# Attention with slot routing on one core: all attention products as plain fp32 in 64x64 array tiles, logits and slot work once per batch

## The chip, the cores and the metric

The kernel runs on one core of a Trainium2 chip. The metric is the device time of one execution in microseconds (us). TensorE (PE in the profile) does the products, VectorE (DVE) and ScalarE (ACT) the elementwise work, SyncE (SP) issues the DMAs; PEld is TensorE's loading of the stationary operand.

## The reference

Attention with a sigmoid in place of a softmax, followed by a soft mixture of experts over all tokens of all batches (8 batches, 12 heads, 448 tokens, head size 64; 3584 tokens of width 768; 32 slots, 8 experts of 4 slots, hidden width 1024), all in float32:

```python
scores = scale * np.matmul(q, k.transpose(0, 1, 3, 2)) - np.log(S)
attn = 1.0 / (1.0 + np.exp(-scores))
x = np.matmul(attn, v)            # then (B*S, H*D)

logits = x @ phi                  # (3584, 32)
d = softmax(logits, axis=0)       # over all tokens
slot_input = d.T @ x              # (32, 768), 4 rows per expert
slot_out[e] = relu(slot_input[e] @ w1[e]) @ w2[e]
c = softmax(logits, axis=1)       # over the slots
return c @ slot_out
```

The softmax over all tokens is kept as a running maximum and a running sum over the batches.

## The kernel before

*Attention loop* (lines 332 to 365). It runs over 48 pairs of heads (8 batches of 6 pairs). Both heads of a pair lie on the 128 partitions, 64 each. For each pair, `load_qk` brings 448 KB of q and k, `load_v` 224 KB of v. `split` (L122) cuts q and k on DVE into a rounded fp32r part and a remainder; `qk_step` (L133) adds three fp32r products per head for each of four chunks of 112 keys (high by high, high by low, low by high), 64 rows by 112 columns of the array, and lets ACT take the sigmoid (L141). `av_step` (L144) multiplies the result with v in plain fp32, 112 rows by 64 columns, both heads beside one another, adding over the four chunks. `evac` (L151) copies the sum out of PSUM, `turn` (L155) transposes it in 32x32 blocks for the slot job.

In the loop's order, PE does for pair p: the scores, then `logits_job` of pair p-1 (L161: four products that write 32 slots by up to 128 tokens each), then the weighted sums of pair p. DVE then splits pair p+1.

*Once per batch.* `softmax_a`, `softmax_b`, `softmax_r`, `softmax_c` (L169 to L205) work on a batch's logits during the first two pairs of the next batch. `spread` (L207) writes the weights to DRAM (`zd`) and reads them back in another order with four DMAs (`dr`). In the third pair, `slot_job` (L245) does 56 small products in 32x32 tiles (L235) and DVE adds them to `acc`. `last_job` (L256) does the same for the last batch without DRAM.

*Tail* (from L373). `w1_part` and `h_part` do the first expert layer, the `hf` loop the second, and `out_batch` (L476) the combination, whose results go to DRAM by L487.

*Order.* PE, SP, DVE and ACT run in the order in which the program is written. All loads and stores go through SP's one queue: an instruction of it that waits holds up all behind it. Weights come in 128 units of 384 KB through a ring: 56 buffers (`wa`, N_A) are filled during attention by L335, 13 more (`wb`, N_B) lie in the memory that attention leaves, and later units wait until an earlier one was read.

Of the kernel before, what the change touches and what calls it, by code (L numbers as in the profile page):

```python
# [18 lines left out]
P = 128  # L19
CH = 112  # L20
NCH = S // CH
# [6 lines left out]
N_B = 13  # L28
# [5 lines left out]
NLT = B // 2  # L34
# [7 lines left out]
def soft_moe_attention(ctx: ExitStack, tc: tile.TileContext, qk, v, phi, w1, w2, cst, out):  # L42
# [14 lines left out]
    lt_all = cpool.tile([P, NLT, P], F32, name="lt_all")  # L57
# [33 lines left out]
    ps_lg = ctx.enter_context(tc.tile_pool(name="ps_lg", bufs=1, space=PSUM))  # L91
    lg_all = ps_lg.tile([P, 512], F32, name="lg").rearrange("p (b t) -> p b t", b=NLT)
    nc.vector.memset(lg_all, NEG)

    def lg_of(b):
        return lg_all[:, b % NLT, :]

    with ExitStack() as actx:
        ldq = actx.enter_context(tc.tile_pool(name="ldq", bufs=1))
        ldv = actx.enter_context(tc.tile_pool(name="ldv", bufs=2))  # L100
        sp = actx.enter_context(tc.tile_pool(name="sp", bufs=1))
        at = actx.enter_context(tc.tile_pool(name="at", bufs=1))
        xp = actx.enter_context(tc.tile_pool(name="xp", bufs=1))
        bounce = actx.enter_context(tc.tile_pool(name="bounce", bufs=2, space=bass.MemoryType.DRAM))
        ps_sc = actx.enter_context(tc.tile_pool(name="ps_sc", bufs=3, space=PSUM))
        ps_av = actx.enter_context(tc.tile_pool(name="ps_av", bufs=1, space=PSUM))

        qkts, vts, splits, av, xTs, ys, dts, drs = {}, {}, {}, {}, {}, {}, {}, {}
# [7 lines left out]
        def load_v(p):  # L116
            if p < NP:
                t = ldv.tile([CH, NCH, P], F32, name="vt")
                nc.sync.dma_start(t[:], v[p])
                vts[p] = t  # L120

        def split(p, i, z, copy=nc.vector.tensor_copy):  # L122
            if z == 0:
                splits[p, i] = sp.tile([P, 2, S], F32R, name=("qs", "ks")[i])
            dst, src = splits[p, i], qkts[p][:, i * S:(i + 1) * S]
            if z == 0:
                copy(dst[:, 0, :], src)  # L127
            else:
                nc.vector.tensor_tensor(out=dst[:, 1, :], in0=src, in1=dst[:, 0, :].bitcast(F32), op=ALU.subtract)  # L129

        atts = {}

        def qk_step(p, c):  # L133
            qs, ks = splits[p, 0], splits[p, 1]
            sc = ps_sc.tile([P, 2, 512], F32, name="sc")
            for z, y in ((0, 0), (0, 1), (1, 0)):
                for h, r in enumerate(heads):
                    nc.tensor.matmul(  # L138
                        sc[0:CH, h, 0:S], ks[r, z, c * CH:(c + 1) * CH], qs[r, y, :], start=(z + y == 0), stop=(z == 1))
            att = at.tile([CH, 2, S], F32, name=f"att{c}")  # L140
            nc.scalar.activation(att[:], sc[0:CH, :, 0:S], AF.Sigmoid, bias=nbias[0:CH, :], scale=QSCALE)  # L141
            atts[p, c] = att

        def av_step(p, c):  # L144
            if c == 0:
                av[p] = ps_av.tile([P, 512], F32, name="av")
            for h, r in enumerate(heads):
                nc.tensor.matmul(  # L148
                    av[p][r, 0:S], vts[p][:, c, r], atts[p, c][:, h, :], start=(c == 0), stop=(c == NCH - 1))

        def evac(p, copy=nc.vector.tensor_copy):  # L151
            xTs[p] = xp.tile([P, S], F32, name="xT", bufs=3)
            copy(xTs[p][:], av[p][:, 0:S])  # L153

        def turn(p):  # L155
            b, hp = divmod(p, NPR)
            if hp == 0:
                ys[b] = xp.tile([P, NPR, S], F32, name="y")
            nc.vector.transpose(ys[b][:, hp, :], xTs[p][:])  # L159

        def logits_job(p):  # L161
            b, hp = divmod(p, NPR)
            for j in reversed(range(4)):
                n = P if j < 3 else S - 3 * P
                nc.tensor.matmul(  # L165
                    lg_of(b)[32 * j:32 * j + 32, 0:n], phi_sb[:, hp, :], xTs[p][:, j * P:j * P + n],
                    start=(hp == 0), stop=(hp == NPR - 1))

        def softmax_a(b):  # L169
            t1 = small.tile([P, 2, 132], F32, name="t1")  # L170
            zt, ls = t1[:, 0, :], lg_of(b)
# [9 lines left out]
            if b < NLT:  # L181
                nc.vector.transpose(lt_all[:, b, :], ls)
# [8 lines left out]
        def softmax_r(b):  # L191
# [5 lines left out]
        def softmax_c(b):  # L197
            pe = dts[b][:, 1, :]
            if b == 0:
                nc.vector.tensor_reduce(out=mz[:, 1:2], in_=pe[:, 0:P], axis=AX.X, op=ALU.add)  # L200
            else:
# [3 lines left out]
                    out=mz[:, 1:2], in0=mz[:, 1:2], scalar=pe[:, P:P + 1], in1=zb[:], op0=ALU.mult, op1=ALU.add)  # L205

        def spread(b):  # L207
            z = dts[b][:, 0, 0:P]
            nc.vector.transpose(z, dts[b][:, 1, 0:P])
            flat = bounce.tile([P, P], F32, name="zd")  # L210
            nc.sync.dma_start(flat[:], z)
# [16 lines left out]
        def slot_mm(b):  # L228
            sl = [ps_sc.tile([P, 2, 512], F32, name="sc") for _ in range(2)]
            y = ys[b]  # L230
            for c in range(NBK):
                for a in range(4):
                    for j in range(4 if c < 2 else 3):
# [4 lines left out]
                            y[32 * a:32 * a + 32, :, k * BLK:(k + 1) * BLK],  # L238
# [17 lines left out]
        def last_job(b):  # L256
            lg = lg_of(b)
# [5 lines left out]
            pa = ps_sc.tile([P, 2, 512], F32, name="sc")  # L263
            pw = ps_av.tile([P, 512], F32, name="av")

            def warm(n):
                for _ in range(n):
                    nc.tensor.matmul(pw[:, 0:P], ident, ident, start=True, stop=True)
# [7 lines left out]
            nc.tensor.matmul(pa[0:1, 0, 0:P], m1[:, 1:2], ident, start=True, stop=True)  # L276
            warm(2)
            widen(b, pe)
            mrow = small.tile([1, 1, NSLOT], F32, name="mrow")
            nc.vector.tensor_reduce(  # L280
                out=mrow[:], in_=pa[0:1, 0, 0:P].rearrange("o (j s) -> o s j", j=4), axis=AX.X, op=ALU.max)
            unwiden(b, ps_sc.tile([P, 2, 512], F32, name="sc")[:, 0, :])
            for j in range(4):
                nc.tensor.matmul(pa[32 * j:32 * j + 32, 1, 0:1], mrow[:, 0, :], csb[0:1, 0:1], start=True, stop=True)
            warm(1)
            sl = slot_mm(b)
            nc.vector.tensor_tensor(out=cw[:, 2:3], in0=m1[:, 1:2], in1=pa[:, 1, 0:1], op=ALU.subtract)
            nc.scalar.activation(cw[:, 3:4], cw[:, 2:3], AF.Exp)
            nc.vector.tensor_scalar(sw, sel4, cw[:, 3:4], None, op0=ALU.mult)
            total = sp.tile([P, DM], F32, name="qs")  # L290
# [7 lines left out]
            ps = ps_av.tile([P, 512], F32, name="av")  # L298
# [3 lines left out]
            nc.vector.tensor_copy(sT[:].rearrange("p k s -> p (k s)"), ps[:, 0:NKC * NSLOT])  # L302
            nc.vector.tensor_reduce(out=cw[:, 4:5], in_=pe, axis=AX.X, op=ALU.add)
# [13 lines left out]
        load_v(0)  # L317
        nc.sync.dma_start(csb[:], cst)
        nc.sync.dma_start(phi_sb, phi)
        load_v(1)  # L320
        pw = ps_av.tile([P, 512], F32, name="av")
        for _ in range(WARM):
            nc.tensor.matmul(pw[:, 0:WN], acc[:, 0:P], acc[:, 0:WN], start=True, stop=True)  # L323
        dmy = small.tile([1, 1], F32, name="dmy")
        nc.scalar.activation(dmy[:], nbias[0:1, :], AF.Sigmoid)
        split(0, 0, 0)
        split(0, 1, 0, nc.scalar.copy)
        split(0, 0, 1)
        split(0, 1, 1)
        load_qk(1)  # L330

        for p in range(NP):
            b, hp = divmod(p, NPR)
            edge, after, third, fourth = (b > 0 and hp == i for i in range(4))
            while state["next"] < min(N_A, (p + 1) * N_A // 40):  # L335
                load_unit()
            if p > 0:
                evac(p - 1)
            if after:
                softmax_r(b - 1)  # L340
                softmax_c(b - 1)
                spread(b - 1)
            for c in range(NCH):
                qk_step(p, c)
            if p > 0:
                logits_job(p - 1)
                if fourth:
                    turn(p - 3)
                    turn(p - 2)
                if not (after or third):  # L350
                    turn(p - 1)
            if edge:
                softmax_a(b - 1)
                softmax_b(b - 1)
            for c in range(NCH):
                av_step(p, c)
            if p + 1 < NP:
                split(p + 1, 0, 0)
                split(p + 1, 0, 1)
                split(p + 1, 1, 0)  # L360
                split(p + 1, 1, 1)
            load_qk(p + 2)
            load_v(p + 2)
            if third:
                slot_job(b - 1)
        dmx = small.tile([1, 1], F32, name="dmx")
        nc.scalar.activation(dmx[:], atts[NP - 1, 3][0:1, 0, 0:1], AF.Exp)
        evac(NP - 1)
        logits_job(NP - 1)
        turn(NP - 1)  # L370
        finish = last_job(B - 1)
# [55 lines left out]
    def logits_turn(b):  # L427
        nc.vector.transpose(lt_all[:, b % NLT, :], lg_of(b))

# [133 lines left out]
```

## Time and profile before

| what | value |
|---|---|
| three runs, us | 447.48, 447.72, 449.42 (median 447.72) |
| span of the profiled execution, us | 445.2 |
| PE / DVE / ACT busy, us | 405.3 / 224.4 / 215.9 |
| mean granted TensorE clock | 0.971 |
| first score product to end of the last weighted sum, us from the start | 5.16 to 326.64 |
| mean DMA rate over the span | 219 GB/s |

For the profiled execution the page gives its span, the time from its first to its last instruction, and no other time; the runs were measured by themselves. In the rows, a group is a line of the kernel on one engine: its busy time, the mean time of one instruction, and the idle time before it with what ended it. Matmuls overlap one another in the array, so the mean of one is longer than the spacing of two.

### The profile page before, as it was taken

What the parts mean: (1) busy time and instruction counts of PE and PEld (TensorE: products, weight loads), DVE (VectorE), ACT (ScalarE), POOL (GpSimd) and SP (SyncE); (2) the same over time, 40 slices, a digit from 0 to 9 for tenths busy, and PEclk for the clock granted to TensorE, in tenths of its full rate; (3) what the DMA queues carried; (4) which work ended last, traced back from release to release, by engine and by line L of the source; (5) the groups of instructions that cost most, each with busy time, mean ns of one, the idle gap of its engine ahead of it and who ended that gap; (6) DMA issues with size and microseconds to landing.
All of it is one profiled execution on the core that took longest, in us unless ns stands there. A gap on an engine that the chain in (4) does not pass through costs nothing.

```text
span 445.2 us, 9802 instructions
## 1 busy us (share of the span) xinstructions
PE 405.3 (91%) x4026; PEld 208.6 (47%) x4026; DVE 224.4 (50%) x511; ACT 215.9 (48%) x299; POOL 2.4 (1%) x12
## 2 busy tenths in 40 slices
PE   8999999999999999999999999999989988798700
PEld 6554454455554454554554545545545543343500
DVE  3545546556563657455474637475533447351800
ACT  5655645763664556556636736555540115442600
POOL 0000000000000000000000000000011000000000
PEclk9999999999999999999999999999999999989865
DMA  5666646656656565655566655433317999999997
GB/s 180 201 182 217 197 141 214 228 175 197 218 167 194 165 212 195 212 182 186 170 193 230 195 164 197 124 90 128 99 37 254 403 400 402 400 401 399 297 287 234
DMA packets 44541, 97.54 MB, mean 219 GB/s; under 512 B 4688, under 2 KB 16592, under 8 KB 44496
## 3 DMA queue, kind: packets, MB, share of 16 engines
q1 hardware_dynamic: 44496, 96.91, 65.4%
q8 instruction: 32, 0.52, 0.5%
q14 instruction: 13, 0.11, 0.1%
HBM read 85.43 MB, written 11.47 MB: 218 GB/s over the span
## 4 chain that ended last, share of the span: by engine, by line
PE 75%; DVE 8%; DMA 7%; issue 3%; ACT 2%; SPq 1%; DVEq 0%; ACTq 0%
PE av L148 31%; PE sc L138 28%; PE lg L165 4%; PE ph L399 3%; PE sc L235 3%; DMA zd<-t 2%; DMA qkt<-in_qk_dram 2%; DMA wa<-in_w_dram 2%; PE po L506 1%; PE pt L416 1%; PE ph L484 1%; PE av L323 1%; SPq L214 1%; DMA out_dram<-wa 1%; DVE tmp L412 1%
## 5 line engine op out<-in xcount | busy, mean ns | idle before, releaser
L141 ACT ACTIVATE att<-sc,nbias 112x896 f32<-112x896 f32 x192 | 177.8, 1008 | 138.5 <-PE sc L138 138.5
L148 PE MATMUL av<-att,vt 112*64 112x448 f32 x768 | 154.9, 545 | 0.0
L138 PE MATMUL sc<-qs,ks 64*112 64x448 f32 x1152 | 139.7, 379 | 1.7 <-DVE ks L127 1.6
L138 PEld LDWEIGHTS sc<-qs,ks 64*112 64x112 f32 x1152 | 93.4, 172 | 60.2 <-issue 28.5
L148 PEld LDWEIGHTS av<-att,vt 112*64 112x64 f32 x768 | 50.8, 136 | 76.6 <-issue 74.5
L127 DVE CAST qs<-qkt 128x448 fp32r<-128x448 f32 x48 | 18.6, 389 | 91.3 <-DMA qkt<-in_qk_dram 79.0
L153 DVE COPY xT<-av 128x448 f32<-128x448 f32 x48 | 29.9, 623 | 35.3 <-PE av L148 35.2
L129 DVE TENSOR_TENSOR qs<-qkt,qs 128x448 fp32r<-128x448 f32 x48 | 30.0, 625 | 1.6
L129 DVE TENSOR_TENSOR ks<-qkt,ks 128x448 fp32r<-128x448 f32 x48 | 30.0, 625 | 1.6
L159 DVE STREAM_TRANSPOSE y<-xT 128x448 f32<-128x448 f32 x48 | 29.2, 631 | 0.9
L165 PE MATMUL lg<-xT,phit 128*32 128x128 f32 (+1 forms) x384 | 20.4, 271 | 0.7 <-DVE xT L153 0.7
L399 PE MATMUL ph<-wa,sT 128*32 128x256 f32 x336 | 19.6, 381 | 0.4 <-DVE sT L302 0.4
L127 DVE CAST ks<-qkt 128x448 fp32r<-128x448 f32 x47 | 18.1, 386 | 0.0
L235 PE MATMUL sc<-y,dr 32*32 32x192 f32 x896 | 17.6, 330 | 0.1
L484 PE MATMUL ph<-st,wb 128*128 128x384 f32 (+1 forms) x32 | 13.9, 434 | 3.7 <-DVE st L523 3.5
L485 DVE COPY wa<-pt 96x384 f32<-96x384 f32 (+1 forms) x27 | 13.9, 551 | 4.7 <-PE pt L484 4.4
L235 PEld LDWEIGHTS sc<-y,dr 32*32 32x32 f32 x896 | 12.9, 103 | 6.9 <-issue 4.9
L485 ACT COPY wa<-ph 96x384 f32<-96x384 f32 (+1 forms) x27 | 11.8, 478 | 7.6 <-PE ph L484 7.6
L165 PEld LDWEIGHTS lg<-xT,phit 128*32 128x32 f32 x384 | 7.6, 108 | 16.4 <-issue 11.3
L399 PEld LDWEIGHTS ph<-wa,sT 128*32 128x32 f32 x336 | 10.2, 110 | 7.4 <-issue 0.8
L484 PEld LDWEIGHTS ph<-st,wb 128*128 128x128 f32 (+1 forms) x32 | 6.3, 196 | 12.6 <-ACT wa L485 5.4
L484 PE MATMUL pt<-st,wb 128*128 128x384 f32 (+1 forms) x32 | 12.0, 376 | 0.0
(111 smaller groups left out, 176.4 us busy)
## 6 DMA issues: line engine op xcount, KB each, us to landing
wa<-in_w_dram SPq DMA_DIRECT2D x112, 384.0 KB, 7.1
qkt<-in_qk_dram SPq DMA_DIRECT2D x48, 448.0 KB, 3.7
vt<-in_v_dram SPq DMA_DIRECT2D x48, 224.0 KB, 4.0
wb<-in_w_dram SPq DMA_DIRECT2D x16, 384.0 KB, 7.6
out_dram<-wa SPq DMA_DIRECT2D x13, 384.0 KB, 5.2
out_dram<-wa SPq DMA_DIRECT2D x14, 288.0 KB, 5.6
dr<-zd SPq DMA_DIRECT2D x28, 64.0 KB, 2.1
out_dram<-wb SPq DMA_DIRECT2D x3, 384.0 KB, 7.3
```

The costliest lines, as they stand in the source:

```text
L127: copy(dst[:, 0, :], src)
L129: nc.vector.tensor_tensor(out=dst[:, 1, :], in0=src, in1=dst[:, 0, :].bitcast(F32), op=ALU.subtract)
L138: nc.tensor.matmul(sc[0:CH, h, 0:S], ks[r, z, c * CH:(c + 1) * CH], qs[r, y, :], start=(z + y == 0), stop=(z == 1))
L141: nc.scalar.activation(att[:], sc[0:CH, :, 0:S], AF.Sigmoid, bias=nbias[0:CH, :], scale=QSCALE)
L148: nc.tensor.matmul(av[p][r, 0:S], vts[p][:, c, r], atts[p, c][:, h, :], start=(c == 0), stop=(c == NCH - 1))
L153: copy(xTs[p][:], av[p][:, 0:S])
L159: nc.vector.transpose(ys[b][:, hp, :], xTs[p][:])
L165: nc.tensor.matmul(lg_of(b)[32 * j:32 * j + 32, 0:n], phi_sb[:, hp, :], xTs[p][:, j * P:j * P + n], start=(hp == 0), stop=(hp == NPR - 1))
L235: nc.tensor.matmul(sl[a // 2][32 * j:32 * j + 32, a % 2, 0:NPR * BLK], drs[b][32 * a:32 * a + 32, j, c * BLK:(c + 1) * BLK], y[32 * a:32 * ...
L399: nc.tensor.matmul(ph[32 * j:32 * j + 32, uu, :], sT[:, 3 * kh + kc, :], utile[("w1", e, 2 * uu + j // 2, kh)][:, kc * 256:(kc + 1) * 256] ...
L484: nc.tensor.matmul(pf[0:n, 0:HALF], cts[g, i][:, c0:c0 + n], st[:], start=True, stop=True)
L485: (nc.scalar.copy if j == 0 else nc.vector.tensor_copy)(ov[:, j, :], pf[0:n, 0:HALF])
```

## The change

Score and weighted product are both done in plain fp32 in units of 128 keys, each cut into two halves of 64 keys. A unit's four score products use the four 64x64 tiles of the array (two heads by two key halves); its four weighted products use them too, with the key halves in the rows and the heads in the columns. Each key half adds up in a PSUM bank of its own; `evac_a` copies one bank and `evac_b` adds the other. 448 keys are three units and 64 keys; the left-over 64 keys of two pairs form one unit, for which v comes as an extra input `vl`. There are 7 units per two pairs, 168 in all. The split on DVE goes away.

The loop runs over units: the scores of unit i, then the weighted products of unit i-2 (LAG). The logits of a batch are done in one block (`logits_job`) after its last unit, into a score buffer, and copied to SBUF; softmax, `spread` and `slot_job` follow at fixed distances in units (spread at 5, slot job at 10). The transposed x overwrites x in a ring of half batches (`xr`). q/k has three buffers instead of one, the four named buffers for the sigmoid's result become three, the score buffers in PSUM two instead of three; N_B is 11 instead of 13. The combine softmax of all eight batches stands in the w1 loop. The cut diff:

```diff
-CH = 112
-NCH = S // CH
+NFK = 3
+LAG = 2
+W_STEPS = 140
-N_B = 13
+N_B = 11
...
-        ldq = actx.enter_context(tc.tile_pool(name="ldq", bufs=1))
-        ldv = actx.enter_context(tc.tile_pool(name="ldv", bufs=2))
-        sp = actx.enter_context(tc.tile_pool(name="sp", bufs=1))
-        at = actx.enter_context(tc.tile_pool(name="at", bufs=1))
+        ldq = actx.enter_context(tc.tile_pool(name="ldq", bufs=3))
+        ldv = actx.enter_context(tc.tile_pool(name="ldv", bufs=1))
+        at = actx.enter_context(tc.tile_pool(name="at", bufs=3))
...
-        ps_sc = actx.enter_context(tc.tile_pool(name="ps_sc", bufs=3, space=PSUM))
+        ps_sc = actx.enter_context(tc.tile_pool(name="ps_sc", bufs=2, space=PSUM))
...
+        def score(u):
+            p, c = u
             sc = ps_sc.tile([P, 2, 512], F32, name="sc")
-            for z, y in ((0, 0), (0, 1), (1, 0)):
+            for t in range(2):
+                pt, k0 = (p, c * P + t * 64) if c < NFK else (p + t, NFK * P)
                 for h, r in enumerate(heads):
                     nc.tensor.matmul(
-                        sc[0:CH, h, 0:S], ks[r, z, c * CH:(c + 1) * CH], qs[r, y, :], start=(z + y == 0), stop=(z == 1))
...
+                        sc[64 * t:64 * t + 64, h, 0:S], qkts[pt][r, S + k0:S + k0 + 64], qkts[pt][r, 0:S],
+                        start=True, stop=True)
+            att = at.tile([P, 2, S], F32, name="att")
+            nc.scalar.activation(att[:], sc[:, :, 0:S], AF.Sigmoid, bias=nbias[:], scale=QSCALE)
+            atts[u] = att
+
+        def weigh(u):
+            p, c = u
+            att = atts.pop(u)
+            if c == 0 and p % 2 == 0:
+                avs[p] = ps_av.tile([P, 2, 512], F32, name="av0")
+            if c == NFK:
+                avs[p + 1] = ps_av.tile([P, 2, 512], F32, name="av1")
+            for t in range(2):
+                row = slice(64 * t, 64 * t + 64)
+                for h, r in enumerate(heads):
+                    if c < NFK:
+                        o, w = avs[p], vts[p][row, c, r]
+                        start = c == 0 and (p % 2 == 0 or t == 0)
+                        stop = c == NFK - 1 and (p % 2 == 1 or t == 1)
+                    else:
+                        o, w = avs[p + t], vls[p // 2][row, r]
+                        start, stop = t == 1, t == 0
+                    nc.tensor.matmul(o[r, t, 0:S], w, att[row, h, :], start=start, stop=stop)
+
+        def evac_a(p):
+            nc.vector.tensor_copy(x_of(p), avs[p][:, 1, 0:S])
+
+        def evac_b(p):
+            av = avs.pop(p)
+            nc.vector.tensor_tensor(out=x_of(p), in0=x_of(p), in1=av[:, 0, 0:S], op=ALU.add)
...
+        def logits_job(b):
+            lg = ps_sc.tile([P, 2, 512], F32, name="sc")[:, 0, :]
+            logits(lg, b, range(NPR))
+            nc.vector.tensor_copy(lgs[0:96, :], lg[0:96, 0:P])
+            nc.vector.tensor_copy(lgs[96:128, 0:64], lg[96:128, 0:64])
+            softmax_a(b)
...
-            sl = [ps_sc.tile([P, 2, 512], F32, name="sc") for _ in range(2)]
+            sl = [ps_av.tile([P, 2, 512], F32, name="av1"), ps_sc.tile([P, 2, 512], F32, name="sc")]
...
+            early[g + 2 + LAG] = [lambda b=b: logits_job(b)]
+            middle[g + 2 + LAG] = [lambda b=b: softmax_b(b)]
+            late[g + 2 + LAG] = [lambda b=b: turn(b * NPR), lambda b=b: softmax_c(b)]
+            late[g + 4 + LAG] = [lambda b=b: turn(b * NPR + 1), lambda b=b: turn(b * NPR + 2)]
+            late[g + 5 + LAG] = [lambda b=b: spread(b), lambda b=b: turn(b * NPR + 3), lambda b=b: turn(b * NPR + 4)]
+            late[g + 7 + LAG] = [lambda b=b: turn(b * NPR + 5)]
+            late[g + 10 + LAG] = [lambda b=b: slot_job(b)]
+
+        for i in range(len(seq) + LAG):
+            for f in early.get(i, ()):
+                f()
+            if i < len(seq):
+                u = seq[i]
+                score(u)
+                if u[1] == NFK:
+                    load_qk(u[0] + 3)
+                elif u[0] % 2 == 1 and u[1] == NFK - 1:
+                    load_qk(u[0] + 3)
+                while state["next"] < min(N_A, (i + 1) * N_A // W_STEPS):
+                    load_unit()
...
+            for f in middle.get(i, ()):
+                f()
+            if i >= LAG:
+                u = seq[i - LAG]
+                weigh(u)
+                p, c = u
+                if c == NFK:
+                    evac_b(p)
+                    load_vl(p // 2 + 1)
+                elif c == NFK - 1:
+                    load_v(p + 2)
...
+                    evac_a(p)
+                    if p % 2 == 1:
+                        evac_b(p)
+            for f in late.get(i, ()):
+                f()
...
-        if e % 2 == 0:
-            combine_softmax(e // 2)
+        combine_softmax(e)
```

More of the change, by code (lines that the diff above doesn't have):

```diff
@@ L33 @@
 CW = 256
-NLT = B // 2
 NBK = 4
@@ L117, in load_v @@
             if p < NP:
-                t = ldv.tile([CH, NCH, P], F32, name="vt")
+                t = ldv.tile([P, NFK, P], F32, name=f"v{p % 2}")
                 nc.sync.dma_start(t[:], v[p])
                 vts[p] = t
[L122 to L129, printed above, removed]
@@ L137, in qk_step @@
                 for h, r in enumerate(heads):
                     nc.tensor.matmul(
-                        sc[0:CH, h, 0:S], ks[r, z, c * CH:(c + 1) * CH], qs[r, y, :], start=(z + y == 0), stop=(z == 1))
[L140 to L149, printed above, removed]
@@ new lines, in evac_a, with logits @@
+        def evac_a(p):
[3 more added lines that the diff above has]
+            nc.vector.tensor_tensor(out=x_of(p), in0=x_of(p), in1=av[:, 0, 0:S], op=ALU.add)
+        def turn(p):
+            nc.vector.transpose(x_of(p), x_of(p))
+        def logits(lg, b, pairs):
+            for hp in pairs:
+                for j in reversed(range(4)):
+                    n = P if j < 3 else S - 3 * P
+                    nc.tensor.matmul(
+                        lg[32 * j:32 * j + 32, 0:n], phi_sb[:, hp, :], x_of(b * NPR + hp)[:, j * P:j * P + n],
+                        start=(hp == 0), stop=(hp == NPR - 1))
@@ L262, in last_job @@
             cw = small.tile([P, 8], F32, name="cw")
-            pa = ps_sc.tile([P, 2, 512], F32, name="sc")
-            pw = ps_av.tile([P, 512], F32, name="av")
+            pa = lgt[:, 1, :]
+            pw = ps_av.tile([P, 2, 512], F32, name="av0")
             def warm(n):
                 for _ in range(n):
-                    nc.tensor.matmul(pw[:, 0:P], ident, ident, start=True, stop=True)
+                    nc.tensor.matmul(pw[:, 1, 0:P], ident, ident, start=True, stop=True)
             nc.vector.tensor_reduce(out=m1[:, 0:1], in_=lg, axis=AX.X, op=ALU.max)
@@ L275, in last_job @@
             warm(2)
-            nc.tensor.matmul(pa[0:1, 0, 0:P], m1[:, 1:2], ident, start=True, stop=True)
+            nc.tensor.matmul(pa[0:1, 0:P], m1[:, 1:2], ident, start=True, stop=True)
             warm(2)
+            turn(b * NPR + 3)
             widen(b, pe)
@@ L280, in last_job @@
             nc.vector.tensor_reduce(
-                out=mrow[:], in_=pa[0:1, 0, 0:P].rearrange("o (j s) -> o s j", j=4), axis=AX.X, op=ALU.max)
-            unwiden(b, ps_sc.tile([P, 2, 512], F32, name="sc")[:, 0, :])
+                out=mrow[:], in_=pa[0:1, 0:P].rearrange("o (j s) -> o s j", j=4), axis=AX.X, op=ALU.max)
+            unwiden(b, pw[:, 0, :])
             for j in range(4):
-                nc.tensor.matmul(pa[32 * j:32 * j + 32, 1, 0:1], mrow[:, 0, :], csb[0:1, 0:1], start=True, stop=True)
+                nc.tensor.matmul(pa[32 * j:32 * j + 32, P:P + 1], mrow[:, 0, :], csb[0:1, 0:1], start=True, stop=True)
             warm(1)
+            turn(b * NPR + 4)
+            turn(b * NPR + 5)
             sl = slot_mm(b)
-            nc.vector.tensor_tensor(out=cw[:, 2:3], in0=m1[:, 1:2], in1=pa[:, 1, 0:1], op=ALU.subtract)
+            nc.vector.tensor_tensor(out=cw[:, 2:3], in0=m1[:, 1:2], in1=pa[:, P:P + 1], op=ALU.subtract)
             nc.scalar.activation(cw[:, 3:4], cw[:, 2:3], AF.Exp)
             nc.vector.tensor_scalar(sw, sel4, cw[:, 3:4], None, op0=ALU.mult)
-            total = sp.tile([P, DM], F32, name="qs")
+            total = at.tile([P, DM], F32, name="att")
             by_block = total[:].rearrange("p (k a n) -> p k a n", k=NKC, a=4)
@@ L297, in last_job @@
                     op0=ALU.mult, op1=ALU.add)
-            ps = ps_av.tile([P, 512], F32, name="av")
+            ps = ps_av.tile([P, 2, 512], F32, name="av0")[:, 0, :]
             for kc in range(NKC):
@@ L317, in soft_moe_attention @@
         load_v(0)
+        load_qk(1)
+        load_vl(0)
+        load_v(1)
+        nc.sync.dma_start(phi_sb, phi)
         nc.sync.dma_start(csb[:], cst)
-        nc.sync.dma_start(phi_sb, phi)
-        load_v(1)
-        pw = ps_av.tile([P, 512], F32, name="av")
+        load_qk(2)
+        pw = ps_av.tile([P, 2, 512], F32, name="av0")
         for _ in range(WARM):
-            nc.tensor.matmul(pw[:, 0:WN], acc[:, 0:P], acc[:, 0:WN], start=True, stop=True)
+            nc.tensor.matmul(pw[:, 0, 0:WN], acc[:, 0:P], acc[:, 0:WN], start=True, stop=True)
@@ L324, in soft_moe_attention @@
         dmy = small.tile([1, 1], F32, name="dmy")
         nc.scalar.activation(dmy[:], nbias[0:1, :], AF.Sigmoid)
[L326 to L371, printed above, removed]
+        seq = []
+        for r in range(NP // 2):
+            p = 2 * r
+            seq += [(p, c) for c in range(NFK + 1)] + [(p + 1, c) for c in range(NFK)]
+        per_b = len(seq) // B
+        early, middle, late = {}, {}, {}
+        for b in range(B - 1):
+            g = (b + 1) * per_b - 1
+            early[g + 2 + LAG] = [lambda b=b: logits_job(b)]
[5 more added lines that the diff above has]
+            late[g + 10 + LAG] = [lambda b=b: slot_job(b)]
@@ new lines, in soft_moe_attention @@
+        for i in range(len(seq) + LAG):
[10 more added lines that the diff above has]
+                    load_unit()
+            if i == len(seq) - 1:
+                lgt = ps_sc.tile([P, 2, 512], F32, name="sc")
+                nc.vector.memset(lgt[96:128, 0, 64:128], NEG)
+            if i == len(seq):
+                dmx = small.tile([1, 1], F32, name="dmx")
+                nc.scalar.activation(dmx[:], atts[seq[-1]][0:1, 0, 0:1], AF.Exp)
+                logits(lgt[:, 0, :], B - 1, range(NPR - 1))
+            for f in middle.get(i, ()):
[9 more added lines that the diff above has]
+                    load_v(p + 2)
+                    if p == NP - 1:
+                        turn(p - 5)
+                        turn(p - 4)
+                    evac_a(p)
[3 more added lines that the diff above has]
+                f()
@@ L373, in soft_moe_attention @@
+        logits(lgt[:, 0, :], B - 1, [NPR - 1])
+        turn(NP - 4)
+        finish = last_job(B - 1, lgt)
     state["wpb"] = ctx.enter_context(tc.tile_pool(name="wpb", bufs=1, reuse_waits="tile"))
@@ L386, in soft_moe_attention @@
     ps_h = ctx.enter_context(tc.tile_pool(name="ps_h", bufs=2, space=PSUM, reuse_waits="tile"))
-    ps_t = ctx.enter_context(tc.tile_pool(name="ps_t", bufs=3, space=PSUM, reuse_waits="tile"))
+    ps_t = ctx.enter_context(tc.tile_pool(name="ps_t", bufs=4, space=PSUM, reuse_waits="tile"))
     ps_o = ctx.enter_context(tc.tile_pool(name="ps_o", bufs=2, space=PSUM, reuse_waits="tile"))
```

79 lines of the change are left out of this document (31 added, 48 removed).

## The prediction

> **What bounds the kernel now.** I read the page first, then the stage table, then the chain of waits around one batch. Busy time and slices of the page:
>
> ```profile
> span 445.2 us, 9802 instructions
> PE 405.3 (91%) x4026; PEld 208.6 (47%) x4026; DVE 224.4 (50%) x511; ACT 215.9 (48%) x299; POOL 2.4 (1%) x12
> PE   8999999999999999999999999999989988798700
> PEclk9999999999999999999999999999999999989865
> DMA  5666646656656565655566655433317999999997
> ```
>
> Two stages are seen. In slices 1 to 30 (attention) PE is full, at full granted clock, and the DMA engines are half idle; from slice 32 the DMA engines are full. The stage table, from the first score product (5.16) to the end of the last weighted sum (326.64), and for one stretch of the tail:
>
> ```profile
> 5.16:326.64 321.48, 319.68 (x3081) 162.86 (x3080) 175.29 (x369) 182.91 (x208) 0.00 (x0) 1.00 0.57 179
> 362.00:400.00 38.00, 31.11 (x263) 13.60 (x256) 20.27 (x65) 16.24 (x46) 0.00 (x0) 0.96 1.03 401
> ```
>
> PE is busy 319.7 of 321.5 us of attention; the tail runs at 401 GB/s with a DMA share of 1. So attention is worth what PE's work is worth, and the tail starts when attention ends. The chain of waits shows how PE's time is made up (start, duration, what):
>
> ```profile
> 5.16 3.33 PE sc L138 x19
> ...
> 62.40 2.12 PE sc L235 x97
> 64.53 2.81 PE sc L138 x24
> 67.34 0.36 PE lg L165 x5
> 67.69 3.16 PE av L148 x16
> 70.85 1.19 PE sc L138 x9
> ...
> 104.59 2.84 PE sc L138 x24
> ...
> 323.43 3.18 PE av L148 x16
> 326.64 0.64 DVE xT L153
> 327.32 0.42 PE lg L165 x5
> ```
>
> One pair of heads costs 70.85 - 64.53 = 6.32 us: scores 2.81, logits 0.36, weighted sum 3.16. A batch is six pairs and one slot job (2.12): 40.06 us (64.53 to 104.59).
>
> **What an fp32 product costs, by itself and beside others.** Groups of instructions, and the weight loads of the weighted sum in order of time:
>
> ```profile
> L148 PE MATMUL av<-att,vt 112*64 112x448 f32 x768 | 154.9, 545 | 0.0
> L235 PE MATMUL sc<-y,dr 32*32 32x192 f32 x896 | 17.6, 330 | 0.1
> L399 PE MATMUL ph<-wa,sT 128*32 128x256 f32 x336 | 19.6, 381 | 0.4 <-DVE sT L302 0.4
> ```
> ```profile
> 8.86 0.14 PEld L148 LDWEIGHTS av<-att,vt 112*64 112x64 f32 x2 [0.23 <-issue]
> ...
> 10.73 0.14 PEld L148 LDWEIGHTS av<-att,vt 112*64 112x64 f32 x2 [0.23 <-issue]
> ```
> ```profile
> 342.70 2.73 PE ph L399 x48
> ```
>
> 768 instructions over 48 pairs are 16 for 8 products: a plain fp32 product is two passes. From 8.86 to 10.73 lie five steps: 0.374 us for each, with two loads, so one pass of 448 columns takes 0.374 us and both heads (two column tiles) run in it at once, the loads hidden. Do four tiles run at once? In L399 four column tiles stand side by side: a pass of 256 columns is 0.374 x 256/448 = 0.214 us, and 48 passes take 2.73 us in the chain, so 48 x 0.214 / 2.73 = 3.8 run at once. In the slot job (rows and columns both cut, 32x32) a pass of 192 columns is 0.160 us and 896 take 17.6 us: 8.2 at once, over four row groups. So rows with four column streams, and rows with both cuts, both exceed what four 64x64 tiles ask for.
>
> **The change part by part.** *Score and weighted sum.* A pair now has 3.5 units; each has four score products and four weighted products, 16 passes of 448 columns. Four at once: 16/4 x 0.374 = 1.496 us a unit, 168 units: 251.3 us. Both kinds have the same tile shape, so the change of shape that now costs 3.16 - 8 x 0.374 = 0.17 us per block goes away between them. What could pace a unit instead is ACT:
>
> ```profile
> L141 ACT ACTIVATE att<-sc,nbias 112x896 f32<-112x896 f32 x192 | 177.8, 1008 | 138.5 <-PE sc L138 138.5
> L153 DVE COPY xT<-av 128x448 f32<-128x448 f32 x48 | 29.9, 623 | 35.3 <-PE av L148 35.2
> L129 DVE TENSOR_TENSOR qs<-qkt,qs 128x448 fp32r<-128x448 f32 x48 | 30.0, 625 | 1.6
> L159 DVE STREAM_TRANSPOSE y<-xT 128x448 f32<-128x448 f32 x48 | 29.2, 631 | 0.9
> ```
>
> One sigmoid of 1.01 us (as many elements per partition as before) per 1.50 us, and two units of lag: hidden; without that lag about 1.2 us a unit would lie open. At the very start unit 2 must wait for unit 0's sigmoid (0.75 + about 1.2 after the first product, against 1.5): 0.5 us once. The split on DVE (four operations per pair) goes, a second evacuation of 0.63 comes: DVE is off the path before and after, as one pair now takes it about 0.63 x 3 = 1.9 us of 5.2.
>
> *Logits.* 24 products per batch in one block: 48 passes of at most 128 columns. Lower bound half of the 2.73 us that 48 passes of 256 columns take; upper bound six of the present blocks, 6 x 0.36 = 2.16. They are shaped like the former: 1.4, and 0.17 to change back: 1.6. Seven batches in the loop 11.2, and five pairs of the last 1.3: 12.5 us.
>
> *Slot job.* Same instructions, 2.12 + 0.17 = 2.3; seven: 16.1 us.
>
> Attention: 251.3 + 12.5 + 16.1 + 0.5 = 280.4 instead of 321.5: **-41.1 us**.
>
> *Round trip through DRAM before the slot job.* It is now issued five units ahead. SP's wait and the DMA table:
>
> ```profile
> SPq L214 <- DMA zd<-t: 22.3, 7, 4.9
> ```
> ```profile
> dr<-zd SPq DMA_DIRECT2D x28, 64.0 KB, 2.1
> zd<-t SPq DMA_DIRECT2D x7, 64.0 KB, 2.8
> ```
> ```profile
> 137.66 0.43 SPq L214
> 138.14 0.43 SPq L214
> ```
> ```profile
> DMA to landing us min/median/max: 1.8/2.1/3.9
> ```
>
> One issue costs SP about 0.43 us; the four reads follow one another at 0.48. Write issue 0.4, SP's wait 22.3/7 = 3.2 (4.9 at most), four reads 1.9, landing 2.1: 7.6 us, 9.3 at most. Ahead of it in the same step stand a load of the q/k pair, which waits for that step's scores, and a weight unit: 0.8. From the end of those scores to the slot job are 0.75 + 5 x 1.50 = 8.25 us. So the middle case is late by 0.15, the worst by 1.85. SP's next loads (v above all) are queued behind the wait; they are used some six units after it, so they have about 12 us. I take 0.7 us per batch: **+5 us**, bounds 0 and 13.
>
> *End of attention.* Two evacuations in a row instead of one: **+0.7**; up to 1.9 if the turns (0.63 each) put into the last job are not covered by ACT and PE.
>
> *Ring.* Two buffers fewer, other places in memory.
>
> ```profile
> 335.86 7.50 SPq L85 DMA_DIRECT2D wb<-in_w_dram  x11
> ...
> 343.91 7.74 SPq L85 DMA_DIRECT2D wa<-in_w_dram  x8
> ```
>
> Of the first 13 wb units 11 wait for the last job's products, two go earlier. With three q/k buffers in front of the stack about four units (3 KB each a partition in 10.5 KB and what follows) come free before the last job's tile. Each (384 KB at 401 GB/s) is 0.98 us of DMA time; eight issues in 7.74 us agree. Bounds: two units gained (-2), two lost (+2); I take **-1**, as loads in the tail follow one another without a break.
>
> Other edits (combine softmax moved into the w1 loop, one more ps_t buffer, later constants) lie under transfers at 401 GB/s; were that cover gone, four more softmax rounds in the w1 loop would cost some 2 us.
>
> Sum: -41.1 + 5 + 0.7 - 1 = -36.4, span 445.2 - 36.4 = 408.8. The median of the runs shown, 447.72, is 2.5 above the profiled span; so I forecast **411 us**.
>
> **The rivals.** *A, slower: the four tiles do not all run together.* Place: every unit. The score products now cut rows as the old ones did (L138), and those are no proof of full overlap:
>
> ```profile
> PEld sc L138 <- ACT att L141: 14.6, 46, 0.3
> ```
>
> 12 steps in 2.81 us are 0.234 a step, against 0.187 for half of the 0.374; of the difference, ACT explains 14.6/48 = 0.3 us a pair, about half. With the whole ratio, 1.25, a unit is 1.87 us and the end 411 + 168 x 0.374 = 474; with two at a time as in L148, 2.99 us: 662. It decides from (321.5 - 29.1 - 5) / 168 = 1.71 us a unit on. Against it speak 3.8 and 8.2 at once. Chance 0.08.
> *B: the round trip is late in each batch.* Landing 3.9 instead of 2.1 and a wait of 4.9: about 3.6 late, seven times 25 us, 20 more than taken: 431. DMA traffic per us rises by 15%, which speaks for it; that a deeper q/k buffer takes pressure off SP, against. Chance 0.14.
> *C: the weight loads lie open.* A load of 0.14 us in front of each of four steps: 168 x 4 x 0.14 = 94, time 505. Against it: the steps at 8.86 to 10.73 leave no room for 0.14. Chance 0.03. By the Trainium skill (TensorE: Matmul & The Clock Gate, section The mechanism) a weight load overlaps a running product only when the row group differs. By that rule C would come; the rows of L148, which all use the same rows and hide their loads, disagree.
> *D, no change: attention shortens but transfers take its place*, with 56 weight units carried in less time. It would need 36 us more DMA time; attention uses 0.57 of it now. Chance 0.03.
>
> The Trainium skill (same page, section Measured speedup vs the span model) gives 3.07 times for four row tiles; by that a unit would be 1.95 us and the end near 487, which is A with a page behind it, while this kernel's 32x32 row exceeds it.
>
> **How the numbers follow.** Forecast 0.72 (404 to 419 by its bounds: 411 less 5 and 2, plus 8), B 0.14, A 0.08, C 0.03, D 0.03. Range 403 to 433: it holds the forecast and most of B. About 0.5% (2 us) is what a measurement of this kernel can tell from no change: faster 0.86, within 0.03, slower 0.11.
>
> **What would show it.** PE groups of the two product lines: a unit's score block near 0.75 us and its weighted block near 0.75, no idle time between; their busy time together near 251 us. The first 64x64 steps spaced by 0.374 with four loads each. PE idle ahead of the slot job tells B. End of the last weighted sum near 291; DMA full from about 300 on. A unit above 1.71 us would make the forecast's sign wrong.

## The result and the profile after

The changed kernel takes 425.71 us (median of four runs, 423.82 to 426.77) against 447.62 us for the kernel before in the same comparison: ratio 0.9522, 95% interval 0.9472 to 0.9572. It is faster by about 22 us; 36 were forecast.

The page of the changed kernel, the rows that answer to those shown of before:

```profile
span 424.5 us, 11237 instructions
PE 377.5 (89%) x4794; PEld 170.1 (40%) x4794; DVE 164.2 (39%) x383; ACT 206.0 (49%) x274; POOL 2.4 (1%) x12
...
PEclk9999999999999999999999999999968998969885
DMA  6667467558736755874665565252309999999987
```

The same two stages are there. Attention now ends at 303.88 instead of 326.64. What is new is the dip of the granted clock just before the DMA engines fill up. The stage table of the changed kernel (columns: length, then busy time and instructions of PE, PEld, DVE, ACT, POOL, then granted clock, DMA share, GB/s), attention and the last job up to the first expert product:

```profile
5.17:303.88 298.71, 286.58 (x3848) 121.55 (x3848) 114.81 (x241) 173.52 (x184) 0.00 (x0) 1.00 0.60 195
```
```profile
303.88:317.50 13.62, 9.25 (x156) 6.82 (x156) 7.06 (x20) 1.24 (x4) 1.93 (x7) 0.75 0.07 25
```

The last job in the kernel before:

```profile
326.64:336.28 9.64, 7.00 (x156) 5.17 (x157) 4.57 (x15) 1.24 (x4) 1.93 (x7) 1.00 0.13 42
```

So the span's 20.7 us are made up of three parts: attention 321.5 to 298.7, that is -22.8; the last job 9.64 to 13.62, +4.0; the rest of the tail 445.2 - 336.28 = 108.9 to 424.5 - 317.50 = 107.0, -1.9. And in attention PE is now idle for 298.7 - 286.6 = 12 us, where before it was idle for 2.

The chain of waits of the changed kernel, at the start and around a batch's edge (start, duration, what):

```profile
5.17 1.75 PE sc L133 x8
6.93 1.02 ACT att L137
8.00 0.98 PE sc L133 x8
...
41.98 1.45 PE sc L173 x30
43.43 0.98 PE sc L133 x8
44.49 1.01 ACT att L137
46.07 0.96 DVE t L207
48.80 0.98 PE av L157 x8
49.78 0.75 PE sc L133 x8
51.28 0.75 PE sc L133 x8
52.03 0.75 PE av L157 x8
53.54 0.75 PE av L157 x8
54.29 0.75 PE sc L133 x8
```

A block of scores and a block of weighted products take 0.75 us each: from 49.78 to 54.29 are three units, 1.503 us a unit, where 1.496 was forecast. The four tiles do run together. But between 43.43 and 48.80 the chain goes over ACT and DVE: PE waits. The timeline of that stretch, DVE and PE:

```profile
46.07 0.95 DVE L207 RECIPROCAL t<-t 128x128 f32<-128x128 f32 x1 [0.86 <-ACT t L202]
46.41 0.93 PE L133 MATMUL sc<-qkt 64*64 64x448 f32 x8
...
47.06 0.29 DVE L208 TENSOR_TENSOR t<-t 128x128 f32<-128x128 f32 x1
47.39 0.31 DVE L209 STREAM_TRANSPOSE t<-t 128x128 f32<-128x128 f32 x1
...
47.62 0.24 DVE L211 TENSOR_REDUCE mz<-t 128x1 f32<-128x128 f32 x1
47.79 0.30 DVE L217 STREAM_TRANSPOSE lt_all<-lgs 128x128 f32<-128x128 f32 x1
48.12 0.62 DVE L160 COPY xr<-av 128x448 f32<-128x448 f32 x1
...
48.80 0.98 PE L157 MATMUL av<-att,vl 64*64 64x448 f32 x8 [1.45 <-DVE xr L160]
```

The weighted products of the left-over keys (`vl`) start right after `evac_a` (L160) has copied the other bank of the same accumulator, and that copy stood on DVE behind `softmax_c`. The scores ahead of it would have let them start at 46.41 + 0.75 = 47.16; they run at 48.80, and their block after the pause takes 0.23 longer (0.98 against 0.75). The view of line L157 counts what its products and their weight loads waited for, and the table of waits parts the two:

```profile
  DVE xr L160: 36.8, 24
```

```profile
PE av L157 <- DVE xr L160: 11.8, 7, 1.7
PEld av L157 <- DVE xr L160: 25.0, 17, 2.5
```

The 24 waits belong to 17 of the 24 left-over units, since a batch edge counts twice. At the seven batch edges the weight loads wait (2.2 to 2.5 us) and PE itself stands idle too (1.45 to 1.7 us); in ten more units only the weight loads come late (0.77 us idle ahead of them instead of 0.22). The seven units right behind a slot job don't wait: the copy is over by then. (As the load side is idle for a part of each unit anyway, the sum of the waits is not their price; that is measured below.)

### The profile page after: what moved, and what is told of

Read it like the earlier page. It is cut to its first block, busy times and chain, and to the rows that moved or that the text cites. A ratio compares the mean times of both kernels' runs of the same rounds, so it can differ in the third digit from the quotient of the medians.

```text
span 424.5 us, 11237 instructions
## 1 busy us (share of the span) xinstructions
PE 377.5 (89%) x4794; PEld 170.1 (40%) x4794; DVE 164.2 (39%) x383; ACT 206.0 (49%) x274; POOL 2.4 (1%) x12
## 4 chain that ended last, share of the span: by engine, by line
PE 77%; DVE 10%; issue 4%; ACT 3%; DMA 1%; DVEq 0%; ACTq 0%
PE av L157 28%; PE sc L133 28%; PE po L528 5%; PE sc L173 3%; PE av L246 2%; PE sc L246 2%; PE ph L510 2%; PE ph L429 2%; DVE t L207 2%; PE pt L446 1%; DVE xr L160 1%; DVE tmp L442 1%; DMA out_dram<-wa 1%; PE pt L484 1%; PE pt L510 1%
## 5 line engine op out<-in xcount | busy, mean ns | idle before, releaser
L137 ACT ACTIVATE att<-sc,nbias 128x896 f32<-128x896 f32 x168 | 169.1, 1007 | 126.8 <-PE sc L133 126.8
L133 PE MATMUL sc<-qkt 64*64 64x448 f32 x1344 | 158.1, 541 | 0.2 <-ACT att L137 0.2
L157 PE MATMUL av<-att,v 64*64 64x448 f32 x1152 | 134.0, 536 | 0.0
L160 DVE COPY xr<-av 128x448 f32<-128x448 f32 x48 | 30.0, 625 | 135.9 <-PE av L157 135.7
L133 PEld LDWEIGHTS sc<-qkt 64*64 64x64 f32 x1344 | 50.1, 134 | 73.2 <-issue 67.1
L157 PEld LDWEIGHTS av<-att,v 64*64 64x64 f32 x1152 | 43.9, 133 | 63.9 <-issue 63.9
L164 DVE TENSOR_TENSOR xr<-xr,av 128x448 f32<-128x448 f32 x48 | 29.8, 621 | 24.2 <-PE av L157 23.4
L157 PE MATMUL av<-att,vl 64*64 64x448 f32 x192 | 23.2, 554 | 11.8 <-DVE xr L160 11.8
L167 DVE STREAM_TRANSPOSE xr<-xr 128x448 f32<-128x448 f32 x48 | 28.1, 621 | 1.1 <-PE sc L173 1.1
L246 PE MATMUL sc<-xr,dr 32*32 32x192 f32 x448 | 17.7, 355 | 0.0
L246 PE MATMUL av<-xr,dr 32*32 32x192 f32 x448 | 17.4, 354 | 0.0
L157 PEld LDWEIGHTS av<-att,vl 64*64 64x64 f32 x192 | 6.4, 131 | 27.4 <-DVE xr L160 25.0
L246 PEld LDWEIGHTS av<-xr,dr 32*32 32x32 f32 x448 | 10.8, 108 | 6.4 <-issue 5.2
```

The lines of the kernel that those rows point to most:

```text
L133: nc.tensor.matmul(sc[64 * t:64 * t + 64, h, 0:S], qkts[pt][r, S + k0:S + k0 + 64], qkts[pt][r, 0:S], start=True, stop=True)
L137: nc.scalar.activation(att[:], sc[:, :, 0:S], AF.Sigmoid, bias=nbias[:], scale=QSCALE)
L157: nc.tensor.matmul(o[r, t, 0:S], w, att[row, h, :], start=start, stop=stop)
L160: nc.vector.tensor_copy(x_of(p), avs[p][:, 1, 0:S])
L164: nc.vector.tensor_tensor(out=x_of(p), in0=x_of(p), in1=av[:, 0, 0:S], op=ALU.add)
L167: nc.vector.transpose(x_of(p), x_of(p))
```

## The experiments

Every kernel below does the whole computation. Ratios are to the kernel before of the same comparison; a time is a median.

**Which wait is it?** Two readings were open: that the two banks of the even pair's accumulator `av0`, being one tile, make the write to one wait for the copy out of the other; or that the odd pair's accumulator `av1`, allocated at this point, is handed over late.

First, `av0` as two tiles of one bank:

```diff
-                avs[p] = ps_av.tile([P, 2, 512], F32, name="av0")
+                avs[p] = [ps_av.tile([P, 512], F32, name=n) for n in ("av0", "av2")]
...
-                    nc.tensor.matmul(o[r, t, 0:S], w, att[row, h, :], start=start, stop=stop)
+                    nc.tensor.matmul(o[t][r, 0:S], w, att[row, h, :], start=start, stop=stop)
...
```

> The even pair's accumulator av0 becomes two one-bank tiles; nothing else changes. Theory (the product of the left-over keys waits for the copy of av0's other bank, because both banks are one tile): all 24 waits of L157 on the copy L160 go, 17 of about 0.23 us and 7 at batch edges of about 1.9 us, 17 us together; time near 409 us. Rival (the wait comes from taking over av1, placed in DVE's order at the point where av1 is allocated): nothing moves, 425 us, and the waits stay.

Measured: 409.67 us, ratio 0.9164 (0.9122 to 0.9206). The view of the weighted products (now L158) names no DVE wait any more, and the stage table shows PE busy 282.4 of 282.8 us of attention:

```profile
  issue: 68.6, 308
  DMA wa<-in_w_dram: 0.4, 2
```
```profile
5.17:288.01 282.84, 282.39 (x3848) 127.43 (x3840) 114.74 (x240) 173.43 (x184) 0.00 (x0) 1.00 0.64 206
```

Attention shrank from 298.71 to 282.84: the wait cost 15.9 us. Of these, 11.7 are idle time of PE (12.1 to 0.4) and 4.2 are busy time (286.6 to 282.4), as the 17 blocks behind a wait are no longer drawn out: 17 x 0.23 = 3.9. (The expectation counts 24 waits, 17 of them short; it is 17 with ten short ones.)

Second, `av1` allocated earlier:

```diff
-            if c == NFK:
+            if p % 2 == 0 and c == (NFK if p % NPR == 2 else 0):
                 avs[p + 1] = ps_av.tile([P, 2, 512], F32, name="av1")
```

> av1 is allocated two or three units earlier (at the pair's first unit), but in the pairs beside a slot job, where it stays. Theory (av0 as one tile): nothing moves, 425 us. Rival (the take-over of av1): 16 of the 24 waits go, all those at batch edges among them: 7 x 1.9 + 9 x 0.23 = 15 us, time near 410 us.

Measured: 425.41 us, ratio 0.9522 (0.9482 to 0.9561), and the waits stay:

```profile
  DVE xr L160: 36.7, 24
```

The edit moves the allocation in 16 of the 17 units that wait. So it is the shared tile, not the hand-over.

**Why is it long at batch edges?** `softmax_c` one unit later, behind the copy:

```diff
-            late[g + 2 + LAG] = [lambda b=b: turn(b * NPR), lambda b=b: softmax_c(b)]
+            late[g + 2 + LAG] = [lambda b=b: turn(b * NPR)]
+            late[g + 3 + LAG] = [lambda b=b: softmax_c(b)]
```

> softmax_c of a batch is issued one unit later on DVE, behind the copy of the first pair's bank instead of ahead of it. Theory (PE waits for that copy, which stands behind 2.5 us of softmax work on DVE): the seven waits at batch edges shrink from about 1.9 to 0.23 us, 11.5 us together, time near 414 us; the other 17 waits stay. Rival (the copy is late because of something else on DVE, or the slot job becomes late, as its weights leave DVE later): less than 4 us gained, or PE idle before the slot job.

Measured: 413.07 us, ratio 0.9237 (0.9196 to 0.9279), 12.6 us less than the changed kernel. The same 17 units still wait, but all of them only with their weight loads, 0.77 us each, and PE stands idle in none. But now the slot job waits for its weights from DRAM, which it did not before (views of L157 and of L246):

```profile
  DVE xr L160: 13.1, 17
```
```profile
  DMA dr<-zd: 4.5, 6
```

So the order on DVE made the long waits, and the round trip through DRAM had hardly any slack: a later softmax uses it up.

**The last job.** Six more warm products (products whose result nobody reads, there to keep PE at work) between the last weighted sum and the last logits:

```diff
...
+        pw = ps_av.tile([P, 2, 512], F32, name="av0")
+        for _ in range(6):
+            nc.tensor.matmul(pw[:, 1, 0:P], ident, ident, start=True, stop=True)
         logits(lgt[:, 0, :], B - 1, [NPR - 1])
```

> Six more warm products between the last weighted sum and the last pair's logits. Theory (the granted clock fell to 0.67 in the last job since PE stood idle for 1.4 us while two evacuations ran and was thinly used after it): the clock stays near 1, the last slot products take about 2.0 instead of 3.2 us and the first expert products 1.5 instead of 2.7, the tail starts about 3 us earlier, time near 422.5 us. Rival (the clock falls for another reason, or the tail's transfers do not start earlier): within 1 us of 425.7.

Measured: 423.71 us, ratio 0.9483 (0.9434 to 0.9532): the interval overlaps that of the changed kernel. In its profile the clock held up to the first expert product:

```profile
303.72:315.10 11.38, 8.28 (x169) 6.49 (x169) 7.00 (x20) 1.24 (x4) 1.92 (x7) 1.00 0.09 34
```

But the kernel with the earlier `av1`, which changes nothing in this place, had a high clock over its last job too, and took no longer for it:

```profile
304.76:316.01 11.25, 6.80 (x156) 5.15 (x156) 6.99 (x20) 1.24 (x4) 1.92 (x7) 1.00 0.10 36
```

In both profiles the clock falls right behind the last job, to 0.77 over the first 96 expert products. So where it falls differs from execution to execution, and this run doesn't show that these warm products prevent it.

A second try, on the kernel with two tiles for `av0`, put warm products into three gaps (six before the last logits, six ahead of the product of the slot sums, two behind it):

```diff
...
             sl = slot_mm(b)
+            warm(6)
...
+            warm(2)
             nc.vector.tensor_copy(sT[:].rearrange("p k s -> p (k s)"), ps[:, 0:NKC * NSLOT])
...
```

> The kernel with av0 as two tiles, and extra warm products in three gaps of the last job: six before the last logits, six while DVE adds up the slot sums, two while the slot inputs are copied. Theory (the low granted clock in the last job comes from PE being thinly used there): clock near 1 through the first expert products, last weighted sum to first expert product 10.5 instead of 13.5 us, time near 406.5 us. Rival (the clock falls anyway, as in the run with six warm products, where only its place moved): within 1 us of 409.7.

Measured: 407.16 us, ratio 0.9126 (0.9094 to 0.9158), against 0.9164 (0.9122 to 0.9206) without: 2.5 us less in the medians, with intervals that overlap. The profiles agree in direction; the last job with two tiles, without and with the warm products:

```profile
288.01:301.50 13.49, 9.48 (x156) 7.02 (x157) 7.16 (x20) 1.24 (x4) 1.92 (x7) 0.74 0.07 27
```
```profile
288.61:299.66 11.05, 10.14 (x185) 8.34 (x185) 7.10 (x20) 1.24 (x4) 1.92 (x7) 1.00 0.09 34
```

2.4 us are gained in the profiled stretch. And in the ten profiles after the change, the clock is 0.74 to 0.78 over the 96 expert products behind the last job in the eight kernels without these three groups of warm products, and 1.00 in the two with them (this one and the last one below); before the change it was 1.00 too. That makes it likely that the low clock comes from a thinly used PE; which of the gaps matters, and how thin is too thin, no run shows.

**What the second unit of lag is worth**, on the kernel with two tiles:

```diff
-LAG = 2
+LAG = 1
```

> The kernel with av0 as two tiles, and the weighted products one unit behind the scores instead of two. Theory (one unit of lag covers the sigmoid: from the end of a unit's scores to its weighted products lie 1.50 us, the sigmoid needs 0.11 + 1.01): no wait in the middle of a batch, only where ACT also does the two softmax operations of 0.3 us each, some 0.5 us per batch: 410 to 414 us. Rival (as the prediction had it, the second unit of lag is what hides the sigmoid): waits of L157 on L137 in most of the 168 units, above 430 us.

Measured: 408.94 us, ratio 0.9157 (0.9099 to 0.9216), no change. Right after a batch's logits its chain has no gap:

```profile
39.98 1.45 PE sc L174 x30
41.43 0.91 PE sc L133 x8
42.34 0.75 PE av L158 x8
43.09 0.75 PE sc L133 x8
43.84 0.75 PE av L158 x8
```

One unit covers the sigmoid. The margin is thin: the weight loads now wait for ACT 152 times, and the products only once, for 0.4 us.

**What the common tile shape is worth**: the scores of full units as two products of 64 rows by 128 columns, on the kernel with two tiles:

```diff
+            for h, r in enumerate(heads) if c < NFK else ():
+                nc.tensor.matmul(
+                    sc[:, h, 0:S], qkts[p][r, S + c * P:S + c * P + P], qkts[p][r, 0:S], start=True, stop=True)
...
```

> The kernel with av0 as two tiles, and the scores of the 144 full units as two products of 64 rows by 128 columns of the array instead of four of 64 by 64: as many passes at once per column of the array, but each unit now changes the shape twice. Theory (a change of shape costs 0.17 to 0.23 us, as seen where logits and slot job stand between units): 144 x 2 x 0.17 to 0.23 = 49 to 66 us more, 459 to 476 us. Rival (the change of shape is not what costs; the 0.2 us seen there are waits for data): within 5 us of 410.

Measured: 458.02 us, ratio 1.0265 (1.0205 to 1.0325): slower than the kernel before. Its chain shows where; L131 is the wide score, L136 the 64x64 one of a left-over unit:

```profile
60.36 0.95 PE sc L131 x4
61.31 0.91 PE av L161 x8
62.22 0.75 PE sc L136 x8
62.98 0.75 PE av L161 x8
63.73 0.95 PE sc L131 x4
64.68 0.91 PE av L161 x8
```

Where the shape changes, a block takes 0.95 or 0.91 us instead of 0.75. (458.02 - 409.67) / 288 changes = 0.17 us each, the 0.17 that the prediction read off the old weighted sum. The 0.16 of the 64x64 block is the change, since the same block takes 0.75 behind its own shape. The wide block never follows its own shape here but in the slow first microseconds, so part of its 0.20 could be its own length. With these two shapes in turn, the change of the kernel would have won nothing.

**What the tail waits for.** In the changed kernel SP's wait table has one long wait: the transfers of weight units (L85) wait for the last job's sum (L307), which lies in a sigmoid buffer:

```profile
SPq L85 <- DVE att L307: 13.7, 1, 13.7
```

On the kernel with two tiles this sum was moved to the third of `xr` that the last batch doesn't use:

```diff
-            total = at.tile([P, DM], F32, name="att")
-            by_block = total[:].rearrange("p (k a n) -> p k a n", k=NKC, a=4)
+            total = xr[:, 1].rearrange("p h s -> p (h s)")[:, 0:DM]
+            by_block = total.rearrange("p (k a n) -> p k a n", k=NKC, a=4)
```

> The kernel with av0 as two tiles, and the last job's sum placed in the free third of xr instead of a sigmoid buffer. Theory (the tail is bound by its transfers, which start when that buffer comes free): three to four more weight units of 0.98 us are loaded before the last job ends, 3 to 4 us less: 406 us. Rival (the tail's start is set by PE's last job, not by loads): within 1 us of 409.7.

Measured: 405.16 us, ratio 0.9082 (0.9038 to 0.9127), 4.5 us less in the medians than with two tiles alone (the intervals just touch). Part of this can be the granted clock, whose mean over a run was 0.957 to 0.973 here and 0.953 to 0.964 there. Eight of the `wb` units are now issued ahead of the wait instead of four, and the wait is down:

```profile
SPq L85 <- DVE xr L308: 8.1, 1, 8.1
```

**All together:** two tiles, the sum in `xr`, the warm products of the second try.

> av0 as two tiles, the last job's sum in xr, and the extra warm products, together. If the last two gains (medians lower by 4.5 and 2.5 us than with the two tiles alone) add up, as one starts transfers earlier and the other shortens the products ahead of them: 402 to 403 us. If both act on the same start of the tail, the larger alone stays: 405 us.

Measured: 404.12 us, ratio 0.9035 (0.8995 to 0.9076). It is the fastest kernel of this study, some 43 us below the kernel before and some 22 below the changed one. It isn't told apart from the one without the warm products, so their gain does not clearly add up with that of the earlier loads.

## Why the prediction was right or wrong

Direction and range were right (425.71 in 403 to 433), the size was not: span -20.7 instead of -36.4. Step by step, in us:

| step of the prediction | forecast | found | from |
|---|---|---|---|
| 168 units at once | 251.3 | 252.5 | 168 x 1.503 |
| start, waiting for the first sigmoid | 0.5 | 1.3 | 8.00 - 5.17 - 2 x 0.75 |
| wait of the left-over products for a copy | none | 15.9 | attention with and without the shared tile |
| round trip ahead of the slot job | 5 | 0 | no wait in the view of the slot products |
| last job | +0.7 | +4.0 | 9.64 to 13.62 |
| tail behind it (ring) | -1 | -1.9 | 108.9 to 107.0 |

-36.4 + 1.2 + 0.8 + 15.9 - 5 + 3.3 - 0.9 = -21.1; 0.4 is left over. Logits and slot jobs were right: with two tiles attention leaves 282.8 - 252.5 - 1.3 = 29.0 us for them, where 12.5 + 16.1 were forecast. At the start the first block of scores takes 1.75 us in the chain instead of 0.75, so the first sigmoid came late.

*The step that failed* is the one on DVE: "DVE is off the path before and after, as one pair now takes it about 0.63 x 3 = 1.9 us of 5.2". The share was about right (DVE is busy 39% of the span) and proved nothing. The work removed from DVE was not on PE's path, while the added copy is, at the point where PE next writes to the tile it reads, one unit later. The diff showed all of it: `evac_a` after a pair's third unit, `softmax_c` ahead of it on DVE, and a fourth unit that writes to the same `av0`. The prediction never asked what PE's next write to `av0` waits for.

*Four at once*: right, and rival A fell. 16 passes of 0.374 in 1.503 us are 3.98 at once. The 3.07 times that the Trainium skill gives for four row tiles (TensorE: Matmul & The Clock Gate, section Measured speedup vs the span model) is not what 64x64 tiles reach here.

*Weight loads hidden*: right, rival C fell: blocks of 0.75 us for two steps leave no time for them. By the rule of the Trainium skill (TensorE: Matmul & The Clock Gate, section The mechanism), loads overlap running products only when the row group differs; here two of the four tiles share their rows, and the trace shows no time for an open load. The loads are hidden only inside a run of such blocks: behind a wait or a change of shape they are not ahead (last section).

*No change of shape between score and weighted sum*: right, and worth more than the prediction said: without it the kernel is slower than before.

*Two units of lag*: the statement that the sigmoid would lie open without them doesn't hold for one unit of lag, which is enough; no run has none.

*Round trip*: SP's wait for the write is 21.0/7 = 3.0 us on average, 3.9 at most, where 3.2 and 4.9 were taken:

```profile
SPq L224 <- DMA zd<-t: 21.0, 7, 3.9
```

So the middle case was near, and the 5 us added for the bad ones did not come. With two tiles for `av0` the slot products (now L247) wait a little, as the view here shows; in the run with the later softmax it was 4.5 us (rival B on a small scale):

```profile
  DMA dr<-zd: 0.4, 2
```

*Transfers in attention* (rival D): it fell, with a DMA share of 0.60 in the shorter attention.

*Last job*: it has two parts. In the two profiles that keep the clock at 1.00 without more warm products (the earlier `av1`, the later softmax) it takes 11.25 us, 1.6 more than before, inside the prediction's bound of 1.9. Of these 0.65 are the second evacuation, and 0.5 are a warm product (L279) that waits while ACT copies the other bank of its tile, a shared tile once more (the table of the run with two tiles, where warm products have a tile of their own, has no such row):

```profile
PE av L279 <- ACT dr L235: 0.5, 1, 0.5
```

The other 2.4 are the granted clock, 0.75 instead of 1.00, which was not foreseen; why it fell stays partly open. *Ring*: right in mechanism; four `wb` units are issued ahead of the last job's wait, as forecast, where it was two before; -1.9 came of it and the rest of the tail together, where -1 was taken.

## What to carry to other kernels

Give small products of alternating kinds one common tile shape of the array: here each change of shape cost 0.17 us, and 288 of them would have eaten the whole gain. An engine that is busy 39% of the time can still hold up the bound engine for 16 us; for every buffer that the bound engine writes to, ask which instruction reads it last and what stands ahead of that reader in its queue. Accumulators in separate PSUM banks are worth separate tiles when one is drained while the other is still written.

## What the runs showed of the hardware that was not expected

After a pause or a change of shape the first block is 0.16 to 0.23 us longer (0.91 to 0.98 instead of 0.75), so a wait costs this even where PE doesn't stand idle, as in ten of the 17 units that wait. The timeline shows what differs. In a run of blocks the first weight loads of a block start some 0.37 us ahead of its products (11.43 and 11.80); behind the copy at 12.80 they start with them (both at 13.48), and so they do behind a change of shape (both at 11.27 in the run with the wide scores). That the loads explain all of it is not tested.

The granted clock fell to 0.75 in the last job, with PE busy 9.25 of 13.62 us and its longest wait there 1.4 us; in other profiles with the same last job it fell only behind it.
